# Batch 0's pooled v summed by TensorE, loads held by a backlog limit, and the first layer started chunk by chunk

## The chip, the cores and the metric

One core of a Trainium2 chip runs the whole program. The metric is the device time of one execution in microseconds; the profiles give the span from the first to the last instruction, which is a little shorter. TensorE is written PE, VectorE DVE, ScalarE ACT, GpSimd POOL and SyncE SP. Each engine takes its instructions in program order.

## The reference

Three parts follow each other: an attention over q, k, v of 4 batches x 8 heads x 576 positions x 64, and two MoE layers over 2304 tokens of width 512.

```python
q_d = q.reshape(B, H, S // 4, 4, D).mean(axis=3)      # k_d, v_d alike
out_d = sm_attn(q_d, k_d, v_d)                        # 144 x 144 scores
out_up = np.repeat(out_d, 4, axis=2)
mask = np.abs(pos[:, None] - pos[None, :]) < 4
out_local = softmax(where(mask, scale * q @ k.T, -1e9)) @ v
x = (out_up + out_local).transpose(0, 2, 1, 3).reshape(2304, 512)
h = x @ w_in;  x = (h * sigmoid(h)) @ w_out           # w_in 512 x 2048
h = x @ w_in2; out = elu(h) @ w_out2
```

## The kernel before, in words

**Attention.** The work is cut by batch and by pair of heads (four pairs a batch, function `attend`). For a pair, q and k come from memory as rows (L488), are transposed on PE (L527) and copied to SBUF by ACT or DVE (L551 to L557). DVE sums groups of four positions of them for the pooled part (L612). The local scores are 20 small matmuls (L570; the trace has two records for each of these fp32 matmuls, so it counts 40) for two heads in ten windows of 64 keys; DVE scales and masks them (L582) and takes the maximum (L589), POOL subtracts it (L591), ACT takes the exponential (L595), DVE sums and inverts (L599 to L601), POOL multiplies (L605), PE transposes the result (L683), ACT copies it (L692), and 20 matmuls (L750, again 40 records) multiply it with v, which lies in SBUF as the same windows of 64 rows ("vw", loaded by L498 and L502). The pooled part is scores (L622), maximum (L634), exponential (L641), inversion (L647 on ACT, L648 on DVE), scaling on POOL (L651), transposes (L705), copies (L715), and matmuls (L727) with the pooled v. The pooled v is made from a second load of v (L492: the same rows again, 2 KB of four positions in a row, one DMA of 144 KB a head), which POOL adds up in two steps (L662, L663). ACT repeats each pooled result four times (L734), and DVE adds local and pooled into x32 (L760, "join", one for each half of 288 tokens).

**First layer.** x is split into a high and a low part (ACT L793 into xh, POOL L796 into xl), and so are the weights (ACT L822 into wh, POOL L826 into wl); the product is three matmuls per chunk of 128 of the contraction: xh by wh, xl by wh and xh by wl. A group of the first product (L845) is four chunks, 12 matmuls, for one block of 256 tokens and one slice f of 128 hidden values; the second product (L883) has 12 matmuls as well, after tanh (ACT L865), DVE L866, ACT L867 (gh) and POOL L869 (gl). The weights come as 64-bit words, of which ACT and DVE make fp32 (L368, L372 on ACT; L376, L379, L383 on DVE), in loads of 512 KB into three buffers "ws" (w_in by L344, w_out by L349). The first stage of the layer takes the slices f below 8, so 16 loads; x of batch 0 feeds it from about 54 us on, while the pairs of batch 1 and later are put between its groups. From about 347 us to the end other stages run, which the change leaves alone apart from their names of lines.

**What sets the order.** A planner in Python writes the program before it runs. Every step is a `Job` with an engine, an estimated duration, predecessors, the tiles that it takes and uses (`Slots`, `Hold`), and a due time; `pick` takes the job that can start first by the planner's own clocks, and among those within 0.1 us the one due first. So a change of a number moves instructions on every engine.

```python
def fill(t):
    gap = t - clock_of["P"]
    if banks.free:
        filler(min(int((gap - 0.1) / 0.22), 40))
```

Until the first group of the first layer is written, `fill` puts filler matmuls (L320: zeros, bf16, 128x512) where the planner sees PE without work. A filler writes a free PSUM bank, so it waits for the last reader of that bank.

```python
if n == 0 and f < SPLIT_F:
    p1 = Job("P", 8 * T_MM, lambda: first([(c, 0, m) for c in range(KC) for m in range(2)], True, False), xj + [wi_[0]], ...)
    p2 = Job("P", 4 * T_MM, lambda: first([(c, 1, 0) for c in range(KC)], False, True), [p1, wi_[1]], due=due1, lat=0.25)
```

The first three groups are cut in two: 8 matmuls that need xh and xl of all four chunks (all four pairs of heads) and wh, then 4 that need wl.

Of the kernel before, what the change touches and what calls it, by code (L numbers as in the profile page):

```python
# [22 lines left out]
def attention_moe_moe2_kernel(ctx, tc, q, k, v, wi1, wo1, wi2, wo2, out):  # L23
    nc = tc.nc
# [29 lines left out]
    LATE, FRAC = 2.0, (0.5, 0.7, 0.85, 1.0)  # L54
# [22 lines left out]
    cpool = ctx.enter_context(tc.tile_pool(name="cpool", bufs=1))  # L77
# [12 lines left out]
    ident = cpool.tile([P, P], F32, name="ident")  # L90
    mask = cpool.tile([P, NW // 2, WIN], F32, name="mask")
# [29 lines left out]
    serial = [0]  # L121

# [48 lines left out]
    class Job:  # L171

        def __init__(self, eng, dur, fn, preds=(), gate=None, due=1e9, port=False, lat=0.1, other=None, takes=(), uses=(), dma=None):
            self.eng, self.dur, self.fn, self.gate, self.other = eng, dur, fn, gate, other
            self.port, self.lat, self.end, self.due = port or eng == "G", lat, None, 1e9
            self.takes, self.uses, self.dma = list(takes), list(uses), dma
# [28 lines left out]
        def start(self):  # L205
            if self.gate is not None and self.gate not in events:
                return None
            t = events.get(self.gate, -1e9)
            if self.port:
                t = max(t, clock_of["port"])  # L210
            for p in self.preds:
                if p.end is None:
                    return None
                t = max(t, p.end)
# [3 lines left out]
            for slots, kinds in wanted.items():  # L218
                x = slots.can(kinds)
                if x is None:  # L220
                    return None
                t = max(t, x)
            if self.other:
                eng, dur, fn = self.other
                if max(t, clock_of[eng]) + dur + PREFER.get((self.eng, eng), 0.0) < max(t, clock_of[self.eng]) + self.dur:
                    self.other = (self.eng, self.dur, self.fn)
                    self.eng, self.dur, self.fn = eng, dur, fn
            return max(t, clock_of[self.eng])

        def emit(self):  # L230
# [5 lines left out]
            if self.eng == "P":  # L236
                if filling[0]:
                    fill(t)
                now[0] = t + self.dur
# [18 lines left out]
    def pick(limit=1e18):  # L258
# [12 lines left out]
        for job in cand:  # L271
            if job.eng == eng or job.other and job.other[0] == eng:
                x = job.start()
                if x is not None and x <= s and job.eng == eng:
                    ties.append((job.due, job.serial, job))
# [63 lines left out]
    def load_w(i):  # L339
        layer, f, which = order[i]  # L340
        src = wsrc[layer][which].bitcast(I32)
        st = stage.tile([P, 2 * DM], I32, tag="ws", name="ws", bufs=WS_N)
# [8 lines left out]

    landed = {}
    decoded = {}

    def decode_jobs(i, out, preds, takes=(), temp=None):
# [7 lines left out]
        if i not in landed:  # L363
            landed[i] = Job("S", 0.55, lambda: load_w(i), [decoded[i - WS_N]] if i >= WS_N else [], dma=1.75)
# [21 lines left out]
        a = Job("A", 0.62, first, list(preds) + [landed[i]], takes=list(takes) + inner)  # L386
        a2 = Job("A", 0.66, half, [landed[i]])
        b = Job("V", 0.70 if inner else 0.45, second, [a])
        c = Job("V", VEC_[DM], third, [b, a2], port=not inner)
        d = Job("V", VEC_[DM], fourth, [c] + ([decoded[i - 1]] if i - 1 in decoded else []), port=not inner, uses=inner)  # L390
# [14 lines left out]
    wrows = [[wpool.tile([P, DM], F32, tag=tag, name="rows2") for tag in ("wh0", "wl0")] for _ in range(NPAIR)]  # L405
# [33 lines left out]
    VR0 = Slots([tuple(x) for x in wrows])  # L439
    VR = Slots([(natv[:, :DM], natv[:, DM:])])  # L440
# [5 lines left out]
    QK0 = Slots([column(pr, S, 2 * S) for pr in range(NPAIR)])  # L446
    QKD0 = Slots([column(pr, 3 * S, 2 * SD) for pr in range(NPAIR)])
    VD0 = Slots([column(pr, 3 * S + 2 * SD, 4 * D) for pr in range(NPAIR)])
# [3 lines left out]
    MX = Slots([fresh(att, [P, NW], f"mx{n}") for n in range(4)])  # L452
    SM = Slots([fresh(att, [P, 4], f"sm{n}") for n in range(4)])
    NM = Slots([fresh(att, [P, 2], f"nm{n}") for n in range(4)])
    rl2s = [fresh(att, [P, 2 * NW], f"rl2{n}") for n in range(3)]
# [968 lines left out]
```

## Time and profile before

| what | value |
|---|---|
| device time, median of 3 runs | 906.93 us (906.91 to 907.88) |
| the profiled execution | 905.92 us, span 904.1 us |
| PE busy | 885.2 us of the span (98%) |
| DVE, ACT, POOL busy | 630.5, 538.0, 274.9 us (70%, 60%, 30%) |
| mean granted TensorE clock | 0.992 |
| bytes moved by DMA | 101.25 MB, mean 112 GB/s |

PE's "busy" counts fillers too, and a matmul that runs at the lower clock is as busy as one at the higher. The granted clock is a share of 2.4 GHz, so 0.50 is the level of 1.2 GHz.

### The profile page before, as it was taken

To read this page: it belongs to the slowest core of one execution; us is meant where nothing else is said; L and a number is where in the kernel's file an instruction comes from. 1 tells how busy PE (TensorE), PEld (TensorE's weight loads), DVE (VectorE), ACT (ScalarE), POOL (GpSimd) and SP (SyncE) were. 2 spreads that over 40 slices of the span, in tenths; PEclk is the share of its full clock that TensorE was granted. 3 is DMA by queue.
4 is the path that set the end of the run, shared out by engine and by line. 5 is a ranking of instruction groups with operands and counts; after the bars stand their busy time and mean duration, and the time that the engine had idled before them with its cause. 6 is when DMAs were issued, how large, how long until landed. Compare 5 with 4: busy or idle time off the path is not lost.

```text
span 904.1 us, 17255 instructions
## 1 busy us (share of the span) xinstructions
PE 885.2 (98%) x6673; PEld 823.2 (91%) x6673; DVE 630.5 (70%) x1145; ACT 538.0 (60%) x1221; POOL 274.9 (30%) x304
## 2 busy tenths in 40 slices
PE   8889899999999999999999999999999999999998
PEld 5669789999999999999999999898898898998986
DVE  5788864445446987978948988579679888383562
ACT  4677664454555757738448478378388585471650
POOL 5787695665640101310105213001032113010000
PEclk9899999999999999999999999999999999999999
DMA  9885446226108331446153051340430530220301
GB/s 183 213 235 156 101 118 159 78 67 173 31 11 280 123 105 66 157 165 185 47 175 105 36 169 53 105 158 18 154 104 1 198 128 36 88 88 36 105 1 70
DMA packets 106401, 101.25 MB, mean 112 GB/s; under 512 B 62416, under 2 KB 89040, under 8 KB 106320
## 3 DMA queue, kind: packets, MB, share of 16 engines
q1 hardware_dynamic: 103952, 99.57, 37.3%
q8 instruction: 52, 0.85, 0.4%
q10 hardware_dynamic: 2368, 0.59, 0.4%
q14 instruction: 29, 0.24, 0.1%
HBM read 76.55 MB, written 23.59 MB: 111 GB/s over the span
## 4 chain that ended last, share of the span: by engine, by line
PE 86%; DVE 3%; POOL 2%; DMA 1%; issue 1%; ACT 0%; DVEq 0%; SPq 0%; POOLq 0%; ACTq 0%
PE b L1185 29%; PE b L1275 22%; PE b L1273 11%; PE b L883 9%; PE b L845 9%; PE b L750 2%; DMA ws<-in_moe_w_out_dram 1%; PE b L527 1%; PE b L727 1%; PE b L683 1%; PE b L705 1%; PE b L622 1%; PE b L570 0%; DVE wf L383 0%; POOL xl L796 0%
## 5 line engine op out<-in xcount | busy, mean ns | idle before, releaser
L883 PE MATMUL b<-gh,wh 128*128 128x256 f32 x288 | 84.7, 294 | 0.0
L883 PE MATMUL b<-gl,wh 128*128 128x256 f32 x288 | 81.9, 284 | 0.0
L883 PE MATMUL b<-gh,wl 128*128 128x256 f32 x288 | 81.8, 284 | 0.0
L845 PE MATMUL b<-xh,wh 128*128 128x256 f32 x288 | 74.4, 291 | 0.4 <-DVE t L866 0.4
L1275 PE MATMUL b<-wl,grw 128*128 128x512 f32 x192 | 74.8, 389 | 0.0
L1275 PE MATMUL b<-wh,glk 128*128 128x512 f32 x192 | 74.8, 389 | 0.0
L1275 PE MATMUL b<-wh,ghk 128*128 128x512 f32 x192 | 74.7, 389 | 0.0
L1275 PE MATMUL b<-wh,grw 128*128 128x512 f32 x192 | 74.7, 389 | 0.0
L1185 PE MATMUL b<-xhr,wSA 128*128 128x384 f32 x288 | 74.5, 334 | 0.0
L845 PE MATMUL b<-xl,wh 128*128 128x256 f32 x288 | 72.3, 283 | 0.7 <-POOL xl L796 0.7
L845 PEld LDWEIGHTS b<-xh,wh 128*128 128x128 f32 x288 | 55.0, 191 | 2.6 <-DVE t L866 0.8
L883 PEld LDWEIGHTS b<-gh,wh 128*128 128x128 f32 x288 | 55.5, 193 | 1.9 <-issue 1.3
L845 PEld LDWEIGHTS b<-xl,wh 128*128 128x128 f32 x288 | 55.1, 191 | 1.1 <-POOL xl L796 1.1
L883 PEld LDWEIGHTS b<-gl,wh 128*128 128x128 f32 x288 | 55.7, 193 | 0.0
L883 PEld LDWEIGHTS b<-gh,wl 128*128 128x128 f32 x288 | 55.5, 193 | 0.0
L979 DVE TENSOR_TENSOR xlr<-xraw,xhr 128x768 fp32r<-128x768 f32 x47 | 45.4, 970 | 12.5 <-ACT xhr L976 12.3
L1238 DVE SCALAR_TENSOR_TENSOR part<-b,part 128x384 f32<-128x384 f32 (+1 forms) x42 | 24.6, 612 | 40.0 <-PE b L1275 27.1
L1185 PEld LDWEIGHTS b<-xhr,wSA 128*128 128x128 f32 x288 | 52.1, 188 | 0.0
L372 ACT ACTIVATE ws<-ws 128x512 uint32<-128x512 uint32 x64 | 43.2, 674 | 13.5 <-DMA ws<-in_moe_w_out_dram 10.6
L1197 ACT COPY hg<-b 128x384 f32<-128x384 f32 x54 | 25.5, 479 | 42.6 <-PE b L1185 41.8
L865 ACT ACTIVATE t<-b 128x256 f32<-128x256 f32 x72 | 27.5, 382 | 37.0 <-PE b L845 35.3
L976 ACT CAST xhr<-xraw 128x768 fp32r<-128x768 f32 x54 | 44.8, 835 | 7.4 <-DVE xraw L1046 2.6
(279 smaller groups left out, 2792.0 us busy)
## 6 DMA issues: line engine op xcount, KB each, us to landing
ws<-in_moe_w_in_dram SPq DMA_DIRECT2D x32, 512.0 KB
ws<-in_moe_w_out_dram SPq DMA_DIRECT2D x32, 512.0 KB
xraw<-x SPq DMA_DIRECT2D x24, 384.0 KB
xd<-x SPq DMA_DIRECT2D x4, 1152.0 KB
yp<-yo SPq DMA_DIRECT2D x9, 512.0 KB
x<-part SPq DMA_DIRECT2D x6, 768.0 KB
yp<-yo SPq DMA_DIRECT2D x6, 768.0 KB
part<-yp SPq DMA_DIRECT2D x6, 768.0 KB
```

Of the source, the lines that this page charges most:

```text
L372: nc.scalar.activation(st[:, :, 0].bitcast(U32), st[:, :, 0].bitcast(U32), AF.Copy, scale=2.0 ** -29, bias=2.0 ** -10 - 0.5)
L750: nc.tensor.matmul(bank.tile[j * D:(j + 1) * D, o:o + n], vw[j * WIN:(j + 1) * WIN, w, :], aT()[j * WIN:(j + 1) * WIN, w // 2, c0:c0 + n], ...
L845: nc.tensor.matmul(ph.tile[:, :NB0], w[a][:, c, :], x_slot(n, c, b_), start=start and m == 0, stop=stop and m == len(products) - 1,)
L865: th = Job("A", ACT_[NB0], lambda: nc.scalar.activation(tt(), h(), AF.Tanh, scale=0.5), [p2], takes=[t], uses=[ph])
L883: nc.tensor.matmul(y[d // 2].tile[:, o:o + NB0], w[m // 2][:, sl], gg(m % 2), start=f == 0 and m == 0 and d % 2 == 0, stop=fin and m == 2, ...
L976: a = Job("A", ACT_[width], lambda: nc.scalar.copy(hi(), src), preds, gate)
L979: other=("V", VEC_[width], lambda: nc.vector.tensor_tensor(lo(), src, hi().bitcast(F32), ALU.subtract)),
L1185: nc.tensor.matmul(acc_, a[:, cs], b[:, c, :], start=fresh and c == 0 and m == 0, stop=c == 1 and m == 2, skip_group_check=True,)
L1197: snap[after, j] = [Job("A", ACT_[NB], lambda dst=dst, acc_=acc_: nc.scalar.copy(dst, acc_), [], gate, due=soon)]
L1238: nc.vector.scalar_tensor_tensor(dst, src, sc, dst, op0=ALU.mult, op1=ALU.add)
L1273: nc.tensor.matmul(y[d][:, :NB], wm[:, sl], gm, start=first, stop=last_)
L1275: nc.tensor.matmul(y[d], gm[:, sl], wm, start=first, stop=last_)
```

## The change

1. For batch 0 the second load of v and POOL's additions go. POOL writes a matrix of ones and zeros once (`pool_matrix`: a memset and six selects, in the tile natv that later batches use for v) and DVE copies it to the other 64 partitions; for each pair 22 matmuls (L655) multiply it with the windows of v that the local part has loaded anyway, and two copies (L664, 72x128) bring the sums to SBUF. Batches 1 to 3 load and add as before.
2. The planner holds a load back until its own estimate of the DMA backlog is under 3 us, and the three ws buffers are handed out by it.
3. For the first two blocks of 256 tokens and f < 4 a group of the first product is four jobs of 3 matmuls, each of which needs the x of one pair of heads alone.
4. The pooled result is not repeated in SBUF: ACT copies 144 columns (L865) and the join reads each four times (L894). ACT's step L647 becomes one on DVE (L797, 72x4).
5. Due times: the second halves of batch 0's tokens are due at 40 us and later, the first halves at 14; batches 2 and 3 every 14 us; the waits of batch 1's joins on batch 0 are written as predecessors. Some constants moved.

Lines are named by the kernel in which they stand; the same step has other numbers after: L527 is L601, L570 L712, L622 L765, L705 L839, L683 L818, L727 L857, L734 L865, L750 L884, L760 L894, L845 L983, L883 L1031, L320 L328, L488 L554, L498 L564, L826 L964, L796 L935, L715 L845, L552 L630.

```diff
-    LATE, FRAC = 2.0, (0.5, 0.7, 0.85, 1.0)
+    PACKED, PE_POOLED, HALVED, CHUNKED, STICK, T_SECOND = 0, 1, 0, 4, 0.0, 40.0
+    BACKLOG = 3.0
+    LEND = 0
+    SOON, W_EARLY, W_AT = 14.0, 0, -3.0
+    LATE, FRAC = 1.0, (0.25, 0.5, 0.75, 1.0)
...
             t = events.get(self.gate, -1e9)
-            if self.port:
-                t = max(t, clock_of["port"])
+            if self.dma is not None:
+                t = max(t, clock_of["dma"] - BACKLOG)
...
+    def pool_matrix():
+
+        m = pooler()
+        nc.gpsimd.memset(m[:WIN], 1.0)
...
+        nc.vector.tensor_copy(m[WIN:P], m[:WIN])
...
+            def pool_v():
+                vw = hw.tile.rearrange("p (n d) -> p n d", d=D)
+                for n, (w, c) in enumerate(POOLED_BY):
+                    for j in range(2):
+                        rows_ = slice(j * WIN, j * WIN + pool_rows(w))
+                        nc.tensor.matmul(
+                            bankv[j].tile[:HS, c * D:(c + 1) * D], pooler()[rows_, n, :], vw[rows_, w, :],
+                            start=n == 0, stop=n == len(POOLED_BY) - 1, skip_group_check=True,
+                        )
+
+            psv = Job("P", 1.3, pool_v, [lw], lat=0.2, takes=bankv, uses=[hw, hpool], mode="s")
...
-        if n == 0 and f < SPLIT_F:
+        if n < 2 and f < CHUNKED:
+            mine = []
+            for c in range(KC):
+                p2 = Job(
+                    "P", 3 * T_MM, lambda c=c: first([(c, 0, 0), (c, 0, 1), (c, 1, 0)], c == 0, c == KC - 1), [xj[c], wi_[1]] + mine[-1:],
+                    due=due1 - (KC - 1 - c) * 3 * T_MM, takes=[ph] if c == 0 else [], lat=0.25,
+                )
+                mine.append(p2)
+        elif n == 0 and f < SPLIT_F:
...
-                attend(i, 14.0 + 6.0 * pr)
+                attend(i, (14.0 + 4.0 * pr, T_SECOND + 4.0 * pr))
```

On SP, before, the loads of batch 0's third and fourth pair stand like this, between the start and the first weight ("rows" are buffers for q and k and, numbered, for v; "yo" holds windows of v):

```order
L488 DMA rows<-in_k_dram 96x6x64 x2
L492 DMA rows_101<-in_v_dram 72x512
L492 DMA rows_102<-in_v_dram 72x512
L498 DMA yo<-in_v_dram 64x9x64
L502 DMA yo<-in_v_dram 64x64
L498 DMA yo<-in_v_dram 64x9x64
L502 DMA yo<-in_v_dram 64x64
L492 DMA rows_103<-in_v_dram 72x512
L492 DMA rows_104<-in_v_dram 72x512
L498 DMA yo<-in_v_dram 64x9x64
L502 DMA yo<-in_v_dram 64x64
```

The same place on SP after the change:

```order
L554 DMA rows<-in_k_dram 96x6x64 x2
L564 DMA yo<-in_v_dram 64x9x64
L568 DMA yo<-in_v_dram 64x64
L564 DMA yo<-in_v_dram 64x9x64
L568 DMA yo<-in_v_dram 64x64
L564 DMA yo<-in_v_dram 64x9x64
L568 DMA yo<-in_v_dram 64x64
L564 DMA yo<-in_v_dram 64x9x64
L568 DMA yo<-in_v_dram 64x64
L352 DMA ws<-in_moe_w_in_dram 128x4x256
```

The 72x512 loads of v are gone, two at this place for each pair and eight in all, and the first weight moves up behind the windows.

On PE, before, this stands where the first group of the first layer begins (nat_115 and nat_116 are q and k of batch 1, b_90 the group's bank; L750 is the local part of batch 0's last pair, both halves of its tokens):

```order
L750 MATMUL b_89<-spare,yo 64x57 x6
L750 MATMUL b_89<-spare,yo 64x56 x2
L750 MATMUL b_89<-spare,yo 64x61 x2
L527 MATMUL b_94<-ident,nat_115 128x96 x5
L527 MATMUL b_95<-ident,nat_116 128x96 x5
L527 MATMUL b_89<-ident,nat_115 128x96
L527 MATMUL b_89<-ident,nat_116 128x96
L320 LDWEIGHTS t
L320 MATMUL b_91<-t 128x512
L845 MATMUL b_90<-xh,wh_824 128x256
L845 MATMUL b_90<-xl,wh_824 128x256
```

On PE after the change, where the first group begins (ring_112 holds the scores of the last pair, b_90 the group's bank; the L655 row stands 22 times in all before the group's third chunk):

```order
L328 MATMUL b_90<-t 128x512
L818 MATMUL b_92<-ident,ring_112 128x128 x3
L983 MATMUL b_90<-xh,wh_682 128x256
L983 MATMUL b_90<-xl,wh_682 128x256
L983 MATMUL b_90<-xh,wl_683 128x256
L818 MATMUL b_86<-ident,ring_112 128x128 x2
L983 MATMUL b_90<-xh,wh_682 128x256
L983 MATMUL b_90<-xl,wh_682 128x256
L983 MATMUL b_90<-xh,wl_683 128x256
L884 MATMUL b_92<-spare,yo 64x60 x2
L884 MATMUL b_92<-spare,yo 64x57 x8
L655 MATMUL b_93<-yo,natv 72x64
```

The group's chunks now stand between the last pair's transposes, its local part and its pooled v, of which before nothing was left when the group began.

Further up on PE after the change, some 20 rows before, stand these fillers and the flips of the third and fourth pair (b_88 is a bank that DVE reads for the q of batch 1, L630):

```order
L818 MATMUL b_91<-ident,yo 128x128 x2
L839 MATMUL b_93<-ident,ring_114 72x72 x4
L328 LDWEIGHTS t
L328 MATMUL b_88<-t 128x512
L328 LDWEIGHTS t
L328 MATMUL b_88<-t 128x512
L328 LDWEIGHTS t
L328 MATMUL b_88<-t 128x512
L839 MATMUL b_86<-ident,ring_114 72x72 x4
```

The second L839 stands behind three fillers that write b_88.

## Rows read from the trace of the kernel before

**Rows 1.** The page's first line.

```profile
span 904.1 us, 17255 instructions
```

**Rows 2.** Busy time of each engine in stretches of the span (first line: columns).

```profile
core 0: us, PE busy (x) PEld busy (x) DVE busy (x) ACT busy (x) POOL busy (x), PEclk, DMA share, GB/s
11.30:35.00 23.70, 21.68 (x391) 15.91 (x392) 21.69 (x44) 16.66 (x61) 20.02 (x25) 1.00 1.06 225
35.00:40.00 5.00, 3.84 (x47) 2.93 (x44) 2.12 (x5) 0.00 (x0) 2.19 (x4) 0.67 0.71 153
40.00:45.00 5.00, 4.58 (x63) 3.33 (x62) 2.97 (x8) 3.92 (x8) 2.53 (x4) 0.50 0.76 182
...
54.00:65.00 11.00, 8.84 (x59) 7.53 (x59) 10.64 (x21) 9.97 (x29) 11.00 (x12) 1.00 1.12 291
65.00:100.00 35.00, 34.02 (x381) 32.34 (x381) 32.17 (x55) 26.07 (x63) 25.21 (x25) 1.00 0.55 163
100.00:119.40 19.40, 16.66 (x193) 15.00 (x194) 14.21 (x24) 12.10 (x36) 14.87 (x16) 0.91 0.37 71
119.40:140.00 20.60, 19.36 (x268) 17.60 (x267) 14.70 (x30) 12.59 (x42) 17.78 (x24) 1.00 0.45 119
140.00:347.00 207.00, 206.80 (x2246) 200.65 (x2245) 115.29 (x249) 114.45 (x312) 81.29 (x101) 1.00 0.38 110
```

**Rows 3.** Timeline 37 to 55 us: start, duration, instruction, idle before and releaser.

```profile
37.07 1.35 PE L527 MATMUL b<-ident,nat 96*128 96x96 f32 x7 [1.16 <-DMA nat<-in_k_dram]
...
40.22 0.87 ACT L715 COPY ring<-b 72x288 f32<-72x288 f32 x2 [5.33 <-PE b L705]
...
41.85 0.17 DVE L648 RECIPROCAL sm<-sm 72x4 f32<-72x4 f32 x1 [1.34 <-ACT sm L647]
...
44.69 1.86 PE L320 MATMUL b<-t 128*128 128x512 bf16 x4 [0.42 <-DVE x L760]
...
54.11 0.47 PE L845 MATMUL b<-xh,wh 128*128 128x256 f32 x1
```

**Rows 4.** Timeline of SP's issues, first and last of four v loads, first weight.

```profile
4.54 0.73 SPq L492 DMA_DIRECT2D rows<-in_v_dram  x2
...
5.97 0.73 SPq L498 DMA_DIRECT2D vw<-in_v_dram  x1
...
21.69 0.96 SPq L492 DMA_DIRECT2D rows<-in_v_dram  x2
...
22.69 0.83 SPq L498 DMA_DIRECT2D yo<-in_v_dram  x1
...
25.59 0.59 SPq L344 DMA_DIRECT2D ws<-in_moe_w_in_dram  x1
```

**Rows 5.** Groups of POOL's instructions, 10 to 54 us: busy time, mean ns, idle before.

```profile
L662 POOL TENSOR_TENSOR rows<-rows 72x256 f32<-72x256 f32 x8 | 5.8, 725 | 6.1 <-DMA rows<-in_v_dram 6.0
...
L663 POOL TENSOR_TENSOR x<-rows 72x128 f32<-72x128 f32 x8 | 3.6, 453 | 0.6
```

**Rows 6.** Timeline 12 to 25 us: small matmuls of one pair on PE.

```profile
14.35 0.81 PE L570 MATMUL b<-x 64*64 64x64 f32 x40
...
16.37 0.71 PE L622 MATMUL b<-x 64*72 64x144 f32 x8 [0.24 <-DVE x L612]
...
23.40 1.38 PE L750 MATMUL b<-ring,vw 64*64 64x60 f32 x40
```

**Rows 7.** Packets of the DMA queues, 5 to 20 us and 25 to 37 us.

```profile
DMA packets 9672, 2.94 MB, mean 196 GB/s; under 512 B 9369, under 2 KB 9369, under 8 KB 9671
...
DMA packets 5683, 2.97 MB, mean 247 GB/s; under 512 B 4386, under 2 KB 5410, under 8 KB 5679
```

**Rows 8.** Timeline: waits of PE from 58 to 103 us.

```profile
58.38 0.74 PE L845 MATMUL b<-xh,wl 128*128 128x256 f32 x4 [0.99 <-POOL wl L826]
...
102.22 0.80 PE L705 MATMUL b<-ident,ring 72*72 72x72 f32 x8 [2.53 <-DVE ring L582]
```

**Rows 9.** Chain of waits, near 137 us: start, duration, what.

```profile
136.80 3.26 PE b L845 x27
```

More of the change, by code (lines that the diff above doesn't have):

```diff
@@ L121, in attention_moe_moe2_kernel @@
     serial = [0]
+    mode_of = [None]
     class Slots:
@@ new lines, in attend, with follow, scores @@
+        final = []
+        flips, chain = {}, {}
+        def follow(job, key):
+            if key in chain:
+                job.after([chain[key]])
+            chain[key] = job
+            return job
+        for part, (s0, s1, halves_, outs) in enumerate(parts):
+            start_ = part == 0
+            groups = [g for g in ((0, 3), (3, 5)) if s0 <= g[0] and g[1] <= s1]
+            held = [Hold(banks, "a") for _ in range(2)]
+            def scores(s0=s0, s1=s1, held=held):
+                qT, kT = tT()
+                for w in range(2 * s0, 2 * s1):
+                    o, c = (w % 2) * WIN, (w // 2 - s0) * WIN
@@ L768, in attend, with add_mask @@
-            final.append(Job("V", 0.47, join, [pj, ups], due=due + 0.5 * t, uses=[bank]))
-            x_written[pr, 2 * b + t] = final[-1]
+            psl = follow(Job("P", 0.15 + 0.11 * (s1 - s0) * 2, scores, copies, lat=0.2, takes=held + ([hE] if start_ else []), uses=[hqk], mode="s"), "psl")
+            masked = []
+            for j, bank in enumerate(held):
+                def add_mask(j=j, bank=bank, s0=s0, s1=s1):
+                    nc.vector.scalar_tensor_tensor(
+                        E4(s0, s1)[:, :, j, :], bank.tile[:, :(s1 - s0) * WIN].rearrange("p (s w) -> p s w", w=WIN), BSCALE,
+                        mask[:, s0:s1], op0=ALU.mult, op1=ALU.add,
+                    )
+                masked.append(Job("V", 0.15 + 0.00106 * (s1 - s0) * WIN, add_mask, [psl], uses=[bank]))
@@ new lines, in attend, with out_d @@
+            banku = Hold(banks, "a")
+            m0, m1 = HS * halves_[0], HS * (halves_[-1] + 1)
+            def out_d(banku=banku, m0=m0, m1=m1):
+                for c in range(2):
+                    for j in range(2):
+                        nc.tensor.matmul(
+                            banku.tile[j * D:(j + 1) * D, :m1 - m0], vd()[:HS, 2 * j + c, :], aD()[:HS, 2 * j + c, m0:m1],
+                            start=(c == 0), stop=(c == 1),
+                        )
+            psu = follow(Job("P", 0.3 + 0.0015 * (m1 - m0), out_d, flips_d + pv, lat=0.2, takes=[banku], uses=[hvd, haD], mode="s"), "psu")
```

528 lines of the change are left out of this document (298 added, 230 removed).

## The prediction

> **What bounds the kernel now.** The page [rows 1] gives a span of 904.1 us in an execution of 905.92, and PE is busy for 98% of it; that is a mean over stages with different limits, so I went to the table by stretches. From 140 us on PE has hardly a gap (206.80 us of 207 up to 347) [rows 2], and what runs behind 347 us is not changed. So whatever the change is worth lies in the first 140 us, and there I read four stretches [rows 2].
>
> From 11.3 to 35 us DVE works 21.69 of 23.70 us: batch 0's attention goes as fast as DVE goes, and PE's 21.68 us in the same row are largely fillers. From 35 to 45 us the chain stands. The timeline shows why [rows 3]: PE, in program order, stood at the transposes of batch 1's k until they landed at 37.07 us, the flips of batch 0's fourth pair are behind them, and ACT, which copies those flips, was idle for 5.33 us until 40.22. The granted clock was 0.67 and then 0.50 in these ten microseconds, the latter the level of 1.2 GHz. The first group of the first layer starts at 54.11 us [rows 3]. From 54 to 65 us POOL is busy for all of 11.00 us and DVE for 10.64: x and the weights are split as fast as these two can, PE does 8.84 us of work. Behind that PE is short of work now and then: it loses 0.98 us between 65 and 100, 2.74 between 100 and 119.4, and 1.24 between 119.4 and 140 [rows 2]; the largest piece is 2.53 us before a flip that waits for DVE's mask step [rows 8]. In the stretch of that wait the clock is 0.91, so a further 0.09 x 19.4 = 1.75 us of PE's work is lost there. These four make 0.98 + 2.74 + 1.24 + 1.75 = 6.7 us: what there is to win behind 65 us.
>
> **The loads of v.** SP spends from 4.54 to 5.97 us on the first pair's loads of v and from 21.69 to 22.69 on the last's [rows 4]; for four pairs that is between 4 x 1.00 and 4 x 1.43, so 4.0 to 5.7 us, of which I take 4.4 (the later ones are nearer to 1.00). The first weight, issued at 25.59 [rows 4], and q and k of batch 1 behind it come up by that much on SP's queue, past nothing but the windows. If instead the transfers set the pace, 8 x 144 KB = 1.18 MB take 6.0 us at the 196 GB/s of 5 to 20 us and 4.8 at the 247 of 25 to 37 [rows 7]; and if the loads were hidden, 0. PE waited 1.16 us for k [rows 3], so any advance above 1.16 us removes PE's wait, and with it most of ACT's 5.33.
>
> A rule that speaks against this step: what goes is large packets. Of 9672 packets between 5 and 20 us 9369 are under 512 B [rows 7], those of q, k and the windows, and they stay; the v loads have 2 KB packets. The Trainium skill, "DMA: Bandwidth & Descriptors", section "Specifications", says that line rate wants transfers of at least 512 B, so by it the removed bytes are the cheap ones; the trace agrees as far as the mixed stretch moves 196 GB/s and the one with more large packets 247. At the page's fabric ceiling of 435 GB/s 1.18 MB are an estimated 2.7 us, still above 1.16, and the sum by it would be the same.
>
> **POOL's additions.** Sixteen go, 5.8 + 3.6 = 9.4 us [rows 5]. They lie before 54 us, where DVE is the bound and POOL has 3.7 us idle of 23.7 [rows 2], so I count nothing for them; the bound on the other side is what of the 9.4 us stands in the chain between 35 and 54 us, where POOL is busy less than half the time, so nothing again. The memset and the six selects that make the matrix have no row; they run while POOL had to wait for the first rows of v (6.0 us of waiting for them all told [rows 5]). They delay something only if they take longer than that and the first maximum is ready.
>
> **The 88 matmuls.** No row shows them. The nearest are 20 local scores at 0.81 us for the set, 0.041 each, from below; the pooled scores, four in 0.71 us, 0.178 each, cut to 64 of 144 columns, 0.079, from above; and the local outputs, 20 in 1.38 us, 0.069 each [rows 6], nearest in shape (64 rows against 64 columns). So 22 cost 0.9 to 1.7 us, I take 1.5, and 6.1 for four pairs. Three pairs' share and most of the last's lies before the first groups end, where PE has only fillers otherwise; cover that holds as long as DVE sets the pace. Without it the last pair's 1.5 us would show.
>
> **DVE's small step.** The inversion's addition moves from ACT to DVE: by the reciprocal of the same 72x4, 0.17 us [rows 3], 0.7 us for the four pairs in a stretch where DVE is full. Against it DVE no longer waits for ACT in front of the reciprocal (1.34 us in that row). Both stay inside the next term.
>
> **The start of the first layer.** Batch 0's attention up to the last pair's maximum is on DVE as before. Behind it ACT's 5.33 us and PE's 1.16 go, but the order puts new waits there: the second flips stand behind fillers that write a bank which DVE reads for batch 1's q, much like the filler that waited for DVE at 44.69 [rows 3]. Walking down the new order with the durations of before, I get about 39.8 us for that read, 45.6 for the first chunk of the first group (before: 54.11 for its first matmul), and 51 to 52 for the last pair's first join, hardly earlier than before, since it is the end of the longest chain. So four chunks are issued early but the first two groups end together at about 56 us, in place of one. One group is 12 matmuls of 3.26/27 us, 1.45 us [rows 9]; PE's order then has waits for the third weight's low part, as before (0.99 us at 58.38 [rows 8]). At 65 us I see between 0 and 1 us more useful work done than before, and count 0.
>
> **From 65 to 140 us.** By the new order PE has about 11 us more work ahead of the last of the 16 weights' first use than before (two groups of the second product and one pair of batch 1 more), of which 6.1 are the pooled matmuls: 5 us of cover for the waits there. DVE, whose work before the 16th weight grows by some 5 us in the order and which stood for several microseconds in 35 to 50 us before, comes out even or some microseconds ahead. So I let the waits shrink to the rate of the best part of this stretch, 0.98 us in 35, which for 75 us is 2.1, and add 0.4 for the first waits for low parts: 2.5 us remain of 6.7. Bounds: all of them gone, and all of them back.
>
> **Sum.** 905.92 - 6.7 + 2.5 = 901.7 us for a profiled execution; the median of the runs stands 1.0 above that of before (906.93 against 905.92), so 902.7.
>
> **The rivals.** (1) *The stalls stay.* POOL (11.00 of 11) and DVE (10.64) are full from 54 to 65 us [rows 2], and the change takes nothing from either there; if the splits of the weights set the time at which each group can go, what is issued earlier only waits for the next one, and the same 6.7 us come back. That is 905.9 + 1.0 = 906.9, up to 908.4 with the last pair's 1.5 us. It also holds if the loads of v were hidden and k lands no sooner. For it: DVE's 32.17 of 35 us from 65 to 100. Against: PE hardly waits there (34.02).
>
> (2) *Slower.* The fillers in front of the second flips wait for DVE's read of b_88, PE stands for 2 to 3 us, and the clock falls to 0.50 as it was from 40 to 45 us. Ten microseconds in which PE now has real work, the chunks and the last pair's chain, then run at half speed. A stretch of 5 us at 0.50 costs 2.5 us on the chain to the last join; if the stalls behind stay as well the time is 906.9 + 2.5 = 909.4. It decides from the point at which the last pair's first join comes later than about 54.5 us. For it: that PE's gap of 1.16 us in 35 to 40 stood beside 0.67 and 0.50. Against: the chain was as long before, at the same clock. The Trainium skill ("TensorE: Matmul & The Clock Gate", section "Part 1: The HAM clock gate") says that TensorE runs at half its clock until it has been kept busy and falls back when it idles; the trace agrees, with 0.50 behind the idle time at 35 to 37 us.
>
> (3) *More.* The wait for k goes, the clock stays at 1.00 from 35 to 45 us, and the waits behind 65 us vanish: 6.7 + 2.5 = 9.2 us, 905.9 - 9.2 + 1.0 = 897.7.
>
> **How the numbers follow.** Forecast, with a gain of 2 to 7 us, 0.55; stalls stay 0.20; slower 0.12; more 0.13. A difference of 0.2%, 1.8 us, is about what a measurement of this kernel can tell from none. Under 905.1 fall the forecast and the third rival, 0.68; over 908.7 the second, 0.12; between them the first, 0.20. The range goes from 896.0, a little beyond the third rival since its bounds are open (PE's half-clock time before is larger than the 2.5 us I counted), to 908.5, the end of the first; it leaves out the second rival and the tip of the third.
>
> **What the profile will show.** Right: k of batch 1 is in SBUF before PE asks for it, and ACT's wait of 5.33 us before the flips' copies is under 2; a chunk of the first group runs by 46 us, and both first groups are done by 57; the 22 matmuls take 0.9 to 1.7 us; PE's idle time from 65 to 140 us is under 3 us at a clock of 1.00. Wrong: PE stands behind fillers for DVE at 37 to 40 us with a clock of 0.50 up to 50; the last pair's join comes behind 54 us; or PE has again some 5 us of gaps from 65 to 140 us, with DVE or POOL as releaser.

## The result, and the profile after

The changed kernel takes 915.23 us (median of 5 runs, 914.45 to 916.41) against 907.07 (906.91 to 908.07): a ratio of 1.009 with an interval of 1.0074 to 1.0105. It is 8.2 us slower where 4.2 faster was forecast. The profiled execution has a span of 913.2 us, 9.1 more than before [rows 1].

The table of busy time by stretches, as in [rows 2], of the changed kernel:

```profile
core 0: us, PE busy (x) PEld busy (x) DVE busy (x) ACT busy (x) POOL busy (x), PEclk, DMA share, GB/s
...
35.00:40.00 5.00, 3.24 (x32) 2.06 (x29) 4.38 (x12) 3.26 (x10) 3.29 (x3) 1.00 0.75 163
40.00:45.00 5.00, 3.92 (x50) 2.75 (x49) 2.97 (x6) 3.27 (x8) 1.67 (x3) 1.00 0.58 140
...
54.00:65.00 11.00, 8.06 (x54) 6.84 (x52) 9.67 (x22) 7.92 (x23) 9.79 (x12) 0.72 1.04 237
65.00:100.00 35.00, 33.23 (x379) 30.90 (x378) 25.28 (x41) 21.46 (x57) 23.54 (x26) 0.89 0.58 159
100.00:119.40 19.40, 17.73 (x149) 16.07 (x149) 17.26 (x28) 12.81 (x35) 11.19 (x10) 0.85 0.49 127
119.40:140.00 20.60, 20.51 (x291) 18.95 (x291) 16.54 (x34) 12.31 (x40) 17.98 (x22) 0.98 0.35 94
140.00:347.00 207.00, 204.24 (x2236) 198.41 (x2235) 121.85 (x267) 109.68 (x302) 72.42 (x90) 1.00 0.38 111
```

The clock is at 1.00 from 35 to 45 us, where it was 0.67 and 0.50; but it is low in all four stretches behind 54 us, of which before only one, at 0.91, was [rows 2]. Idle time and clock together: 2.94 us and 0.28 x 11 = 3.1 from 54 to 65; then 1.77 + 1.67 + 0.09 = 3.5 us idle and 0.11 x 35 + 0.15 x 19.4 + 0.02 x 20.6 = 7.2 us of clock up to 140. By the same count the kernel before lost 2.2 us and then the 6.7 of the prediction. From 140 to 347 us PE is now idle for 2.76 us, before 0.20.

Two milestones split the span. The view of one line's instructions (first and last start) has the last matmul of the second product in the first layer's first stage, L1031, at 352.3 us (L883 before: 346.6), 5.7 later; and of the paired stage, the one behind it, L1333, first 341.5 and last 876.4:

```profile
L1031 PE MATMUL b<-gh,wl x288: 278/283/415, 70.1 to 352.3; 128*128 128x256 f32 x144
...
L1333 PE MATMUL b<-xhr,wSS x72: 334/334/334, 358.6 to 876.4; 128*128 128x384 f32 x72
...
L1333 PE MATMUL b<-xhr,wAA0h x36: 333/334/346, 341.5 to 852.1; 128*128 128x384 f32 x36
```

The same lines of the kernel before:

```profile
L883 PE MATMUL b<-gh,wl x288: 278/283/416, 63.1 to 346.6; 128*128 128x256 f32 x144
...
L1185 PE MATMUL b<-xhr,wSS x72: 334/334/335, 353.0 to 866.8; 128*128 128x384 f32 x72
...
L1185 PE MATMUL b<-xhr,wAA0h x36: 333/334/346, 335.8 to 842.6; 128*128 128x384 f32 x36
```

That is 534.9 us for the paired stage, where L1185 took 335.8 to 866.8, 531.0 us. So 5.7 us are lost up to its start and 3.9 inside it, far behind the change; the tail gave 0.5 back.

The timeline at PE's waits, with the instructions of DVE and POOL beside them:

```profile
58.21 0.38 PE L983 MATMUL b<-xh,wh 128*128 128x256 f32 x1 [1.30 <-ACT ring L787]
62.13 1.33 PE L818 MATMUL b<-ident,ring 128*128 128x128 f32 x5 [0.84 <-POOL ring L736]
...
81.21 1.14 POOL L804 TENSOR_TENSOR ring<-ring,small 72x576 f32<-72x576 f32 x1 [0.42 <-ACT wf L383]
81.30 3.79 DVE L391 TENSOR_SCALAR wf<-wf 128x512 f32<-128x512 f32 x1
82.32 1.26 POOL L736 TENSOR_TENSOR ring<-ring,small 128x640 f32<-128x640 f32 x1
83.54 1.27 POOL L964 TENSOR_TENSOR wl<-wf,wh 128x512 fp32r<-128x512 f32 x1
85.95 0.41 DVE L1012 SCALAR_TENSOR_TENSOR t<-t,b 128x256 f32<-128x256 f32 x1
86.41 1.06 PE L601 MATMUL b<-ident,spare 96*128 96x96 f32 x5 [1.77 <-DVE t L1012]
...
108.28 3.42 DVE L394 SCALAR_TENSOR_TENSOR wf<-wf,ws 128x512 int32<-128x512 int32 x1
112.09 0.50 PE L839 MATMUL b<-ident,ring 72*72 72x72 f32 x4 [1.67 <-DVE t L1012]
...
159.04 0.55 PE L818 MATMUL b<-ident,ring 128*128 128x128 f32 x3 [2.57 <-POOL ring L736]
...
389.12 2.16 POOL L1126 TENSOR_TENSOR xlr<-xraw,xhr 128x768 fp32r<-128x768 f32 x1
389.49 2.33 DVE L398 SCALAR_TENSOR_TENSOR raw<-ws,raw 128x512 int32<-128x512 int32 x1
392.52 0.45 PE L1421 MATMUL b<-grw,wh 128*128 128x384 f32 x1 [1.48 <-ACT wh L1124]
```

Three of these six waits have a long step of DVE ahead of them. A decode step of DVE from SBUF to SBUF (0.42 us for L391, 0.69 for L394 and L398, when alone) lasts 2.33 to 3.79 us while POOL runs instructions beside it; this is called a hold below. At 86 and 112 us DVE's small step behind it (L1012) then frees a PSUM bank late; PE, in program order, stands for that bank, and everything behind it on PE stands too. At 392 us it is a weight that is late: ACT rounds it (L1124) only behind the decode step. Ahead of the waits at 58, 62 and 159 us there is no hold: PE stood for ACT's exponential (L787) and for POOL's scaling of the local scores (L736). The kernel before had one wait of the first kind, the 2.53 us of [rows 8]:

```profile
98.92 1.25 POOL L605 TENSOR_TENSOR ring<-ring,rl 128x640 f32<-128x640 f32 x1
...
99.09 2.59 DVE L376 TENSOR_SCALAR wf<-wf 128x512 f32<-128x512 f32 x1
...
100.14 1.25 POOL L826 TENSOR_TENSOR wl<-wf,wh 128x512 fp32r<-128x512 f32 x1
...
101.60 0.87 DVE L582 SCALAR_TENSOR_TENSOR ring<-b,mask 128x320 f32<-128x320 f32 x2
```

A hold alone costs PE little: before, decode steps of 2.06 us at 90.33 and 2.23 at 556.5, and after, one of 2.22 at 566.03, had no wait of PE over 0.5 us behind them.

To compare kernels with different orders I counted **useful work**: all of PE's matmuls but the fillers, each at its pace at the full clock (0.120 us for 128x256, 0.035 a record for L884's, 0.019 for L712's, and so on). The pooled matmuls make 6.9 us of it. At 54 us the changed kernel had done 36.3 us, before 28.0; at 65 us 40.8 and 34.8; at 140 us 105.9 and 102.5; at 340 us 306.2 and 304.9. Without the pooled matmuls it is ahead by 1.4 us at 54, behind by 0.9 at 65, by 3.5 at 140, by 5.6 at 340.

### The profile page after: what moved, and what is told of

It is laid out like the page before. It is cut to its first block, busy times and chain, and to the rows that moved or that the text cites. A ratio compares the mean times of both kernels' runs of the same rounds, so it can differ in the third digit from the quotient of the medians.

```text
span 913.2 us, 17615 instructions
## 1 busy us (share of the span) xinstructions
PE 892.0 (98%) x6838; PEld 832.5 (91%) x6838; DVE 644.7 (71%) x1176; ACT 535.3 (59%) x1216; POOL 254.2 (28%) x273
## 3 DMA queue, kind: packets, MB, share of 16 engines
q1 hardware_dynamic: 103280, 98.39, 36.3%
## 4 chain that ended last, share of the span: by engine, by line
PE 56%; DVE 2%; issue 0%
PE b L1333 26%; PE b L1423 21%; PE b L1421 10%; DVE raw L398 1%; DVE raw L394 0%; DVE wl L1127 0%; DVE part L1386 0%; DVE raw L391 0%; DVE b L1341 0%; DVE hgx L1231 0%; DVE glk L1127 0%; DVE ghk L1127 0%; DVE hg L1231 0%
## 5 line engine op out<-in xcount | busy, mean ns | idle before, releaser
L1031 PE MATMUL b<-gh,wh 128*128 128x256 f32 x288 | 84.5, 293 | 0.0
L1031 PE MATMUL b<-gl,wh 128*128 128x256 f32 x288 | 81.8, 284 | 0.0
L1031 PE MATMUL b<-gh,wl 128*128 128x256 f32 x288 | 81.8, 284 | 0.0
L983 PE MATMUL b<-xh,wh 128*128 128x256 f32 x288 | 77.5, 298 | 1.4 <-ACT ring L787 1.3
L1333 PE MATMUL b<-xhr,wSA 128*128 128x384 f32 x288 | 74.5, 334 | 0.0
L983 PE MATMUL b<-xl,wh 128*128 128x256 f32 x288 | 74.2, 286 | 0.0
L983 PEld LDWEIGHTS b<-xh,wh 128*128 128x128 f32 x288 | 56.1, 195 | 3.4 <-ACT ring L787 1.5
L1031 PEld LDWEIGHTS b<-gh,wh 128*128 128x128 f32 x288 | 55.5, 193 | 1.8 <-issue 0.8
L983 PEld LDWEIGHTS b<-xl,wh 128*128 128x128 f32 x288 | 56.2, 195 | 0.0
L1031 PEld LDWEIGHTS b<-gl,wh 128*128 128x128 f32 x288 | 55.7, 193 | 0.0
L1031 PEld LDWEIGHTS b<-gh,wl 128*128 128x128 f32 x288 | 55.5, 193 | 0.0
L1127 DVE TENSOR_TENSOR xlr<-xraw,xhr 128x768 fp32r<-128x768 f32 x47 | 45.4, 970 | 13.5 <-ACT xhr L1124 13.4
L1333 PEld LDWEIGHTS b<-xhr,wSA 128*128 128x128 f32 x288 | 52.1, 188 | 0.0
L983 PE MATMUL b<-xh,wl 128*128 128x256 f32 x288 | 51.2, 287 | 0.1
L736 POOL TENSOR_TENSOR ring<-ring,small 128x640 f32<-128x640 f32 x30 | 38.1, 1271 | 39.9 <-DVE small L797 17.8
```

The source lines that it names most:

```text
L736: eng.tensor_tensor(E3(s0, s1), E3(s0, s1), col3(h, s0, s1).to_broadcast([P, 2 * (s1 - s0), WIN]), op)
L983: nc.tensor.matmul(ph.tile[:, :NB0], w[a][:, c, :], x_slot(n, c, b_), start=start and m == 0, stop=stop and m == len(products) - 1,)
L1031: nc.tensor.matmul(y[d // 2].tile[:, o:o + NB0], w[m // 2][:, sl], gg(m % 2), start=f == 0 and m == 0 and d % 2 == 0, stop=fin and m == 2, ...
L1127: other=("V", VEC_[width], lambda: nc.vector.tensor_tensor(lo(), src, hi().bitcast(F32), ALU.subtract)),
L1333: nc.tensor.matmul(acc_, a[:, cs], b[:, c, :], start=fresh and c == 0 and m == 0, stop=c == 1 and m == 2, skip_group_check=True,)
```

## The experiments

Theory 1: PE's waits, and the half clock behind them, cost the time, and the waits come from DVE steps held by POOL. Theory 2: DVE, ACT and POOL set the pace, and PE's clock only follows. Theory 3: the pooled matmuls are the cost. The times are medians; each ratio, with its interval, is to the kernel before timed in the same runs, and is not the quotient of two medians.

| kernel | us | ratio (interval) | profiled span |
|---|---|---|---|
| e1_cover | 915.64 | 1.0092 (1.0056 to 1.0128) | 913.7 |
| e5_pool_short | 906.5 | 0.9983 (0.9959 to 1.0006) | 905.0 |
| e3_pool_adds | 910.15 | 1.0043 (1.0018 to 1.0068) | 907.8 |
| e4_no_chunks | 905.88 | 0.9990 (0.9969 to 1.0011) | 906.7 |
| e6_port | 913.42 | 1.0054 (1.0034 to 1.0075) | 912.8 |
| e8_due_batch0 | 911.26 | 1.0036 (1.0022 to 1.0051) | 909.6 |
| e9_nochunk_port | 909.11 | 1.0017 (1.0005 to 1.0029) | 908.3 |
| e11_due_later | 906.23 | 0.9985 (0.9973 to 0.9997) | 905.6 |
| e13_soon_off | 913.06 | 1.0075 (1.0048 to 1.0102) | 907.9 |
| e14_batch1_off | 908.34 | 1.0016 (0.9994 to 1.0037) | 905.4 |
| e15_due_nochunk | 908.05 | 1.0015 (0.9998 to 1.0031) | 905.2 |
| e16_due_pooladds | 907.71 | 1.0012 (0.9995 to 1.0029) | 906.0 |
| e17_xlr_short | 914.97 | 1.0089 (1.0059 to 1.0120) | 915.8 |

**e1_cover.** Fillers at four places, all orders kept (the keys of COVER number PE's jobs):

```diff
+    COVER = {69: 12, 73: 8, 110: 16, 133: 15}
...
+                if pseq[0] in COVER:
...
+                    for _ in range(COVER[pseq[0]]):
+                        nc.tensor.matmul(into, w[:, :P], w[:, :256], start=True, stop=True)
```

> The changed kernel with every engine's order as it is, and 12, 8, 16 and 15 filler matmuls (bf16, 128x256, results unused) put on PE directly ahead of the four instructions that it waited for at 56.9, 61.3, 84.6 and 110.4 us. Theory 1 (PE's gaps and the half clock behind them cost the time): the granted clock stays at 1.00 from 58 to 121 us, where the changed kernel has three stretches of 6.83 us at 0.50, worth about 3.4 us each; the span falls by 7 to 10 us from 913.2, to 903 to 906. Theory 2 (what DVE, ACT and POOL deliver sets the pace, the clock only follows): the waits grow by what the clock gives, span 911 to 914. Theory 3 (the pooled matmuls on PE are the cost): 913, or up to 3 us more for the fillers.

The stretches, with 39 to 50 us added:

```profile
39.00:50.00 11.00, 10.03 (x80) 7.55 (x80) 6.59 (x12) 5.65 (x13) 4.27 (x5) 0.53 0.58 165
54.00:65.00 11.00, 9.02 (x104) 7.65 (x104) 9.13 (x19) 7.47 (x22) 8.24 (x11) 1.00 0.77 183
65.00:100.00 35.00, 34.42 (x419) 31.76 (x417) 30.49 (x51) 23.87 (x62) 27.08 (x29) 1.00 0.68 175
100.00:119.40 19.40, 18.23 (x177) 16.32 (x178) 17.63 (x28) 12.89 (x35) 10.78 (x10) 1.00 0.49 134
```

The clock stays at 1.00 as expected, but the span does not fall. Matmul by matmul against the changed kernel: this execution was 3.3 us behind at 49.5 us, since its clock was low from 39 to 50 us, ahead of the first added filler, where the changed kernel's was not; it was 4.6 behind at the third group (62.84 against 58.21 us, the fillers ahead of it had waited 1.27 us for a bank); from there to 120 us it made 6.1 us good and was 1.5 ahead; behind the wait at 157 us the clock fell again, and it lost that. So the clock held at 1.00 went with 6.1 us made good, less than the 10 of theory 1. It is no clean price of the half clock: the 51 fillers take PE an estimated 6 us (12 of them 1.47 us), part of it in place of waits, and a PE that is late waits less for the others. Where the half clock strikes is not fixed by the order of instructions alone. The total (913.7 us where 903 to 906 was expected) doesn't bear theory 1 out, and the 6.1 us speak against theory 2.

**e5_pool_short.** POOL's subtraction and scaling on fewer columns, orders kept:

```diff
+                n_ = 8 if b and eng is nc.gpsimd else WIN
+                x = E3(s0, s1)[:, :, :n_]
+                eng.tensor_tensor(x, x, col3(h, s0, s1).to_broadcast([P, 2 * (s1 - s0), n_]), op)
...
+                n_ = 18 if b and eng is nc.gpsimd else SD
```

> The changed kernel with its order as it is, but where POOL subtracts the maximum, or scales by the inverse sums, for batches 1 to 3 it does so on an eighth of the columns only (the rest of these tiles stays unscaled, so the attention of these batches is not computed). Theory 1 in its full form (DVE's decode steps of 3.79 and 3.42 us at 81 and 108 us were held by POOL's instructions in a row, PE's gaps at 84 and 110 us and the half clock come from them): these two steps fall under 1.5 us, both gaps and both stretches of 0.50 vanish, span 903 to 907 with the first stretch left. Theory 2 (supply, without such a hold): the two steps stay near 3 us, span 910 to 913. Theory 3: no change, 912 to 914.

```profile
65.00:100.00 35.00, 35.00 (x426) 32.96 (x425) 27.76 (x52) 23.81 (x62) 23.60 (x28) 0.99 0.73 192
100.00:119.40 19.40, 17.56 (x211) 15.79 (x211) 18.07 (x32) 13.60 (x41) 10.69 (x14) 1.00 0.43 111
```

DVE's long steps behind 60 us are now 1.43 us at 83 us and 2.37 at 106: the first as expected, the second above it, with a wait of PE of 0.99 us behind it. PE has no gap from 65 to 100 us, the clock is 0.99 and 1.00 up to 119.4, and the whole kernel is 1.1% faster than the changed one. From 65 to 120 us PE does 52.2 us of useful work in place of 44.9. This is theory 1's mechanism, with the reserve that shorter POOL work also relieves the chains that wait for POOL itself. And the total does not measure what the holds had cost: the paired stage still takes 534.9 us (333.3 to 868.1), and at its start this version is 2.5 us ahead of the kernel before (335.8).

**e3_pool_adds.** The loads of v and POOL's additions back (`PE_POOLED` 0, the four buffers of before).

> The changed kernel with batch 0's pooled v made as before the change (eight loads of v and sixteen additions on POOL; no pooled matmuls), everything else as changed; the planner places the rest anew. Theory 3 (6.6 us of pooled matmuls are the cost): span 906 to 909. Theory 1: the 6.6 us lie under PE's free time, so no gain from them as such; the time goes with PE's idle time and half clock between 54 and 140 us, wherever they fall now, 908 to 918.

1.0043 is between the two, and the span of 907.8 lies in theory 3's range, just under the other's; so the time alone decides nothing. At 54 us it had done 30.2 us of useful work, the changed kernel 36.3 less 6.9, and at 65 us 33.4 against 33.9: up to there the loads and additions cost nothing, and their removal gains nothing. What it gains comes later, 2.1 us by 340 us and 3.3 in the paired stage (531.6 us), where the pooled matmuls are long done: it is the order that differs. So theory 3 falls; e16 below bears this out.

**e4_no_chunks.** `CHUNKED` 0.

> The changed kernel without the chunks (the first groups of the first product are again 8 and 4 matmuls, the first of which need all four pairs' x). If the early chunks are what brings PE out of step with DVE and POOL: span 905 to 909 and fewer than three stretches of half clock from 54 to 140 us. Theory 1 without such a special role of the chunks: 910 to 917, again two to four such stretches, in other places.

The whole loss is gone within the interval (0.9990), and span and number of stretches are as expected if the chunks bring PE out of step. At 54 us it has done 37.5 us of useful work, more than with chunks (36.3): the chunks gain nothing, since the last pair's join, at 52.95 us in the changed kernel, ends both groups anyway. It has two stretches of half clock from 54 to 140 us (granted clock 0.63 from 54 to 65 and 0.74 from 100 to 119.4) in place of three, but they cost as much: 0.37 x 11 + 0.03 x 35 + 0.26 x 19.4 = 10.2 us of clock, against 3.1 + 7.2 = 10.3. Most of its gain comes behind 140 us (the table in the next section), so its time does not show the reason that was expected.

**e6_port** and **e9_nochunk_port.** DVE's first decode step counted as one that shares the way to SBUF with POOL; e9 also without chunks:

```diff
-        b = Job("V", 0.70 if inner else 0.45, second, [a])
+        b = Job("V", 0.70 if inner else 0.45, second, [a], port=not inner)
```

> The changed kernel with one word more: the planner counts DVE's first decode step in SBUF (L391) as one that it must not lay beside an instruction of POOL, as it does for the two steps behind it; the rest is placed anew by it. If the holds of DVE by POOL can be planned away: no DVE step over 2 us from 60 to 140 us, no PE gap over 1 us there behind one, span 903 to 908. If the planner's clock is too far off by then (the third step was counted so already and took 2.33 us at 389 us, the second 3.42 at 108): holds of 2 to 4 us in other places, span 909 to 915.

> The changed kernel without the chunks and with DVE's first decode step counted as in e6_port. e4_no_chunks had a span of 906.7 with one hold of DVE of 3.60 us at 103 us and 10.2 us of half clock behind it. If that hold goes, with 1.5 us of PE's gap and about 5 us of work lost to the clock: span 899 to 903, below the kernel before. If holds come back elsewhere: 904 to 909.

Neither helps as hoped. In e6 the longest such step from 60 to 140 us is 2.06 us (at 88.4), but PE waits 4.02 us at once, and no hold is in it. PE's wait and what stood on DVE ahead of it:

```profile
101.94 0.45 DVE L391 TENSOR_SCALAR wf<-wf 128x512 f32<-128x512 f32 x1
102.31 0.68 DVE L398 SCALAR_TENSOR_TENSOR wf<-ws,wf 128x512 int32<-128x512 int32 x1
102.91 0.68 DVE L394 SCALAR_TENSOR_TENSOR wf<-wf,ws 128x512 int32<-128x512 int32 x1
103.62 0.69 DVE L398 SCALAR_TENSOR_TENSOR wf<-ws,wf 128x512 int32<-128x512 int32 x1
104.23 0.81 DVE L779 TENSOR_REDUCE small<-b 72x2 f32<-72x288 f32 x2
...
106.18 0.37 ACT L787 ACTIVATE ring<-b,small 72x144 f32<-72x144 f32 x1
...
107.05 0.58 PE L983 MATMUL b<-xh,wh 128*128 128x256 f32 x1 [4.02 <-ACT ring L787]
```

DVE works without a break; the pooled maximum (L779) stands behind four decode steps, ACT's exponential behind it and behind three of ACT's own steps for weights, and PE needs the bank that the exponential reads. In e9 it is much the same with L1012 behind five decode steps (one of 1.48 us), for 2.93 us at 100 us, while a hold of 3.03 us at 82.08 had no such wait behind it. So a hold lengthens a wait, but the order on DVE and ACT alone makes one too: theory 1 is too narrow on where the waits come from, and theory 2 is right so far.

**e8_due_batch0.** Batch 0's due times as before.

> The changed kernel with batch 0's due times as before (14, 20, 26, 32 us for both halves of each pair). If putting the second halves later is what costs: more useful work done on PE by 65 us than the changed kernel's 41, span 906 to 910. If where PE's gaps fall decides, and this only moves them: 909 to 917, with as many gaps over 1 us between 54 and 160 us.

911.26 us, at 65 us 39.5 of useful work, no more than the changed kernel: about half of the loss is gone, but not by that step. The gaps moved (3.6 and 3.5 us are now the longest).

**e11_due_later, e13_soon_off, e14_batch1_off.** e13 sets back the due times of batches 2 and 3 (SOON), e14 the constants LATE and FRAC, e11 all three and the due times of the copies of x:

```diff
-    SOON, W_EARLY, W_AT = 14.0, 0, -3.0
-    LATE, FRAC = 1.0, (0.25, 0.5, 0.75, 1.0)
+    SOON, W_EARLY, W_AT = 0.0, 0, -3.0
+    LATE, FRAC = 2.0, (0.5, 0.7, 0.85, 1.0)
...
-            keep_x(b_, max(j.due for j in batch_end[b_]) + (60 if b_ < B - 1 else 5))
+            keep_x(b_, max(j.due for j in batch_end[b_]) + (40 if b_ < B - 1 else 5))
```

This is e11's edit; e13 has the SOON line alone, e14 the LATE line alone. FRAC places batch 1's pairs. LATE does more than the expectation of e14 says: it spaces the groups of the first two blocks, by which their weights are due too:

```python
t_ += 24 * T_MM + share.get(n, 0.0) * (1.0 if n > 1 else LATE if f >= FP // 2 else 2.0 - LATE)
```

> The changed kernel with the due times of batches 1 to 3 and of the copies of x as before the change. Batches 2 and 3 were drawn forward (their last scores end at 243 us, before at 257). If that crowding of DVE and POOL is what costs between 120 and 220 us (PE's gap of 2.6 us at 157 us): this gap goes and the span is 908 to 911. If not: 911 to 916, with the gaps at 57 and 84 us as in the changed kernel.

> The changed kernel with the due times of batches 2 and 3 alone as before (no 14 us raster). e11_due_later, which undid these, batch 1's and those of the copies of x, had a span of 905.6. If the attention of batches 2 and 3, drawn forward, is what takes DVE and POOL away: PE's gap of 2.6 us at 157 us goes, and the useful work done from 120 to 160 us is 41 us, as in e11_due_later, in place of 38; span 906 to 909. If batch 1's due times did it: 911 to 915.

> The changed kernel with batch 1's due times alone as before (LATE 2.0, and the shares 0.5, 0.7, 0.85, 1.0 of the stretch in place of 0.25, 0.5, 0.75, 1.0). If batch 1's attention, due earlier by the change, is what crowds DVE and POOL while 16 weights are made (54 to 100 us): useful work done by 70 us near e11_due_later's 47.9 in place of 45.4, and span 906 to 910. If batches 2 and 3 did it: 911 to 915.

e11 undoes the loss, more than either branch of its expectation allowed (span 905.6), and is the one of 13 versions that is faster than the kernel before beyond its interval, by 0.15%. e13's ratio is 1.0075 and e14's 1.0016: most of it goes with LATE and FRAC, and no run parts these two. e13's profiled execution (910.83 us, the lowest of its four) shows what batches 2 and 3 do: up to 120 us it has the changed kernel's waits (1.30, 0.95, 1.76 and 1.65 us) and half clock, but those at 159 and 392 us are gone and the paired stage takes 531.0 us. In e14's stretches:

```profile
54.00:65.00 11.00, 10.50 (x88) 9.97 (x88) 10.45 (x20) 8.93 (x21) 10.92 (x14) 1.00 0.96 283
65.00:100.00 35.00, 30.72 (x295) 28.42 (x294) 29.91 (x51) 21.84 (x57) 20.94 (x21) 0.90 0.49 141
```

From 54 to 65 us PE works 10.50 of 11 us at the full clock, in place of 8.06 at 0.72, and at 70 us it has done 50.9 us of useful work, not 45.4. Batch 1's first pooled queries and keys (L642) are summed on DVE at 59.6 us in place of 46.8; PE no longer meets that pair's exponential and flips (58.21 and 62.13 us above) between its first groups. Then e14 loses more than the changed kernel did, 4.28 us of idle time from 65 to 100, and gains in the paired stage (531.0 us).

**e15_due_nochunk** and **e16_due_pooladds.** e11 without chunks, and e11 with POOL's additions.

> e11_due_later without the chunks. If the two losses add up (8 to 9 us of the due times, 8 to 9 of the chunks, of which each alone already took nearly all back): no more than 2 us below e11_due_later, span 903 to 906, since both undo the same gaps. If they are separate losses: 897 to 900.

> e11_due_later with batch 0's pooled v by its own loads and POOL's additions, as before the change. If the pooled matmuls on PE lie under free time and the loads and additions that they replace lay under it too: the same within 1.5 us, span 904 to 907. If the loads' removal is worth the 4.4 us of SP's queue: 909 to 911. If the pooled matmuls show: 899 to 903.

Neither is better than e11 (1.0015 and 1.0012 against 0.9985), so what undoing the chunks, the pooling and the due times each gives does not add up. With the due times of before, POOL's additions in place of the pooled matmuls gain nothing: 0.3% the other way, with intervals that nearly touch.

**e17_xlr_short.** All orders kept, one POOL instruction at 389 us on 96 of 768 columns.

> The changed kernel with every engine's order as it is and one instruction of POOL, the split xlr at 389 us in the paired stage (2.16 us, 128x768), cut to an eighth of its columns (the rest of this tile of the second layer's input split stays stale). Theory 1 for the late loss (DVE's decode step of 2.33 us beside it is held by POOL, ACT's wh and PE behind it are late by that): the step falls under 1.2 us, PE's waits of 1.48 and 0.27 us at 392 to 394 us and the half clock behind them go, and the paired stage takes 531 us, as before the change, in place of 534.9. Theory 2 (the weight is late since its load or the steps ahead of it are late): the waits shrink by at most 1 us, paired stage 534 to 535.

```profile
394.74 0.70 POOL L1130 TENSOR_TENSOR xlr<-xraw,xhr 128x96 fp32r<-128x96 f32 x1
...
395.11 0.88 DVE L398 SCALAR_TENSOR_TENSOR raw<-ws,raw 128x512 int32<-128x512 int32 x1
```

DVE's step is 0.88 us, not 2.33, PE's wait of 1.48 is gone, and the paired stage takes 347.1 to 878.9, 531.8 us: 3.1 of the 3.9 us come from one POOL instruction beside one DVE step. The median does not show it (1.0089), with an interval wider than that; in this execution the first 347 us took 5.6 longer than in the changed kernel's, with the clock at 0.56 from 39 to 50 us, 0.80 from 65 to 100 and 0.85 from 119.4 to 140.

## Why the prediction was wrong

**Right, up to 54 us.** PE ran the transposes of batch 1's k at 35.19 us without a wait, and ACT copied the flips at 38.11 us [rows 3 had 40.22]; the filler behind DVE's read of b_88 started at 39.24 after 1.54 us (forecast 39.8); the first chunk ran at 44.63 (45.6); the last pair's first join at 52.95 (51 to 52; before 52.16); the 22 matmuls took 1.65 us (1.5); the step moved to DVE (L797, 72x4) took 1.0 us for the four pairs (0.7), and up to 1.26 for one later pair, at 157.75 us beside POOL, which the prediction did not price. The loads of v were worth 2.3 us on SP's queue, since the first weight was issued at 23.27, not the 4.4 of the prediction; one load of a window stood there for 2.20 us. By e3 the advance was worth nothing in the end, which the range of that term allowed. The half clock that rival 2 put at 40 to 45 us did not come in this execution; it came in those of e1, e5 and e17, which have the same order up to there. One reading was wrong without consequence: of PE's 21.68 us from 11.3 to 35 us the fillers are 5.1, not most.

**Off, at 65 us.** Forecast 0 to 1 us ahead, measured 0.9 behind. I had one wait there, for the third weight's low part, at the 0.99 us of before and nothing for the clock. PE stood 1.30 us at 58.21 for batch 1's exponential and 0.84 at 62.13 for POOL's scaling, and the clock was at its lower level from 58.9, behind the first, to 65.8 us.

**The step that failed: "From 65 to 140 us".** I let the waits shrink from 6.7 us to 2.5, and they grew to 3.5 + 7.2 = 10.7; by this count that is 8.2 of the 13.5 us between the 901.7 forecast for a profiled execution and the 915.23 measured. (By useful work it is 6.8: 4.2 to be won, 2.6 lost.) Two things were wrong in it. The two groups and the pair of batch 1 that stand earlier in the order were counted as 5 us of cover for PE; but PE can use what stands behind a waiting instruction only when that one is served, and a pair of batch 1 is itself a chain through DVE, POOL and ACT that PE meets in order. e14 speaks for it: with that pair later, PE is busy for 2.4 us more at the full clock from 54 to 65 us (LATE moves the groups there too, so this is not shown of the pair alone; from 65 to 140 us itself e14 wins only 1.1). And the 2.53 us wait of [rows 8] went into the sum as one that a lead would cover, put down to DVE's mask step, without the hold of 2.59 us ahead of that step. Holds with a wait of PE behind them come at 81, 108 and 389 us in the changed order (e5 and e17 shorten them), and where there is none a short step that PE's bank hangs on stands behind whole decode steps (e6, e9).

**Not foreseen: 140 us and later.** I held PE full from 140 us on and what runs behind 347 us unchanged. The wait up to 159 us (2.57 us for POOL's L736) and the paired stage's 3.9 us both hang on the order as it fell: the first is gone in e6, e8 and e13 and there with 2.89 us in e14, the second is gone in all four (531.0 us).

**Where the time lies.** Useful work without the pooled matmuls, by profiled execution, that each kernel is ahead of the changed one in a stretch, in us (the last column from the spans of the paired stage; entries are good to about 0.4):

| kernel | up to 65 | 65 to 140 | 140 to 340 | paired stage |
|---|---|---|---|---|
| before | 0.9 | 2.6 | 2.1 | 3.9 |
| e4_no_chunks | 1.2 | 0.7 | 2.6 | 2.2 |
| e11_due_later | 2.3 | 0.9 | 1.6 | 2.8 |
| e14_batch1_off | 5.1 | 1.1 | -2.1 | 3.9 |
| e5_pool_short | -0.9 | 7.5 | 1.7 | 0.0 |

Of the loss 2.6 us lie between 65 and 140, and the orders that undo it give at most 1.1 of them back there; they win elsewhere. Only e5, where POOL does less, gets that stretch back.

**The rivals.** (1) said that the stalls come back: they did, and larger. (2) had the sign and the half clock, but not the place, and its sign that the last pair's join comes behind 54 us did not show. (3) fell.

**What stays open.** No single part of the change explains 8.2 us: undoing the chunks or batch 1's due times, or shortening POOL's steps, each takes back 0.7 to 1.1%, the pooling and batch 0's due times about half of that; they do not add, and they take it back in different stretches. (With batch 1's due times go those of the first groups.) The load limit and the join without the repeat in SBUF were undone in no run. Which gaps a given order has I can read only from its trace. And e1 shows, over the first 49.5 us of an unchanged order, an execution that differs by 3.3 us from the changed kernel's; what decides on that clock stretch I did not find.

## What to carry to other kernels

When a planner's numbers change, read the new order for what PE meets in sequence: work that depends on a chain through three other engines is no cover, it can be the next wait, where the time gained by an earlier start is given back. Price a wait of PE with the half clock behind it, and a SBUF-to-SBUF step of DVE with the POOL instructions beside it, from the places in the trace where they met. And a part that is hidden (here 1.18 MB of loads and 9.4 us of additions) gained nothing by going, while a new order cost 0.9%.

## What the runs showed of the hardware

DVE's decode steps from SBUF to SBUF lasted 0.42 us (L391) or 0.69 (L394, L398) alone and up to 3.79 us beside POOL; with the neighbour cut to an eighth, 0.88 us in place of 2.33. The same steps with an operand in PSUM lasted 0.67 to 0.70 us beside POOL too (16 of them in the changed kernel). The Trainium skill ("GPSIMD Engine Reference", section "1. Specifications") says that POOL shares its SBUF interfaces with VectorE, in contention with DVE instructions in a two-port mode or with two SBUF inputs; the traces agree for L394 and L398, which have two SBUF inputs (3.42 and 2.33 us); L391 has one, and that it runs in a two-port mode is not shown here. They add that even the step of 72x4 elements (L797), 0.10 us alone, took 1.26 beside POOL's 1.26, and that a DVE instruction can stand for three POOL instructions in a row (81.30 us: 3.79 beside 1.14, 1.26 and 1.27). I had not expected the clock's low stretch near 40 to 50 us to come and go between executions of one order: from 39 to 50 us it was 1.00 in the changed kernel's profile, 0.53 and 0.56 in e1's and e17's.
